# A fused linear-attention and MoE kernel: another order inside a seven-product quarter, and four pieces of side work in other places (blocks 2 to 8)

## The chip, the cores and the metric

The kernel runs on one core of a Trainium2 chip. The metric is the device time of one execution in microseconds (us). Before the change three runs gave 275.19, 275.74 and 276.08 us; the median is 275.74. Engines are called as in the profile: PE is TensorE's matmuls and PEld its weight loads, DVE is VectorE, ACT is ScalarE, POOL is GpSimd, and SP issues most of the DMAs.

## What is computed

For each of 8 batches there is linear attention with 8 heads, 576 tokens and head size 64, and after it a gated layer over all 4608 tokens. Inputs and output are float32; the kernel computes its products in bfloat16 and sums them in float32.

```python
phi = where(x > 0, x, exp(x) - 1) + 1              # of q and k
kv  = k_p^T v                                      # per head, summed over tokens
x   = (q_p kv) / (q_p z + 1e-6)                    # z: sum of k_p over tokens; x is [4608, 512]
h   = x @ w_in                                     # 512 -> 2048
g   = h * sigmoid(beta * h)
out = g @ w_out                                    # 2048 -> 512
```

## The kernel before, in words

**Blocks.** The 576 tokens of a batch are nine groups of 64 rows. Eight of the groups of batch b, 512 tokens, are block b (0 to 7). The ninth groups of all batches, 512 more tokens ("odd tokens", kept in `xT_tail`), are block 8. The loop of L1031 goes over blocks 1 to 8; block 0 is written out ahead of it. Each turn has a phase H (`h_phase` for blocks 1 to 3, `h_fast` for 4 to 8) that computes h and g, and a phase Y (`y_fast`) that computes the output. A schedule is written by hand: every engine runs its instructions in the order in which the code issues them, and the compiler adds the waits. The dictionaries `sh` and `sy` hold side work that is called at a numbered step of H or Y: attention of the next blocks, loads, copies.

**H.** The 16 chunks `ff` of 128 hidden features each take four matmuls of 128x512 (`h_mm`, L402) into one bank of the four-deep ring `hps` and one activation (`silu`, L410) that writes the chunk of g. In blocks 4 to 8 a quarter of the features (chunks 0 to 3; in blocks 7 and 8 also 8 to 11) is computed with seven block products in place of eight (`h_products`, L807). It needs sums and differences of `w_in` (`h_w_sums`, L779, four DVE operations of 128x512 for each quarter) and of x (`h_x_sums`, L793). The products go in four parts between plain chunks. `cw` is a tile of two banks ("hc"), `z` is the first bank of another such tile ("hz"); both are from the ring `wps` of two tiles. Part 1 (L834) ends in two DVE additions that read `cw[:,0]` and `z`; part 2 (L840) ends in L842, which reads `cw[:,1]`; part 3 (L844) accumulates into `cw[:,0]`, `cw[:,1]` and `z`, and DVE adds `h_u[0]` into `cw[:,1]` in place (L848) and into `c2[:,0]` from `z` (L849). `out(0)` (L856) has ACT read `cw` for the quarter's first two chunks, `out(1)` reads `c2`, in SBUF, for the other two.

**The banks behind it.** In blocks 4 to 6, H runs `numer_all` (attention of the next block, L319) after chunk 9 and ahead of chunk 10. Its 72 small matmuls (L333) write first 28 into two banks of `hps`, then the rest into two tiles of `wps`; the first of these takes the place of "hc", so it waits for `out(0)`'s reads. Chunk 10's bank is the one that chunk 8's activation has to read out before. In blocks 7 and 8 a second `h_products` follows the first, and its "hc" takes the place of the first's.

**Y.** Seven products of sixteen 128x256 matmuls (L964): pa, pd, pa, pc, pb, pd, pb. Their left sides are halves of g and sums of them: `g_diff` (L722, one DVE operation of 128x1024 for four chunks) and `g_sums` (L726, three each). DVE forms u2 = pc + r1 (L987) and u3 = pd + u2 (L988); the second product into pd may start when u3 has been formed, since u3 reads pd's bank. Between these lies side work on DVE: `phi` of a later batch (L169, L175), `h_x_sums`, `h_w_sums`.

**POOL.** `tail_copy(b)` (L366) copies the odd tokens of block b from `xT`, which a DMA transpose fills. `next_loads(n)` (L1020) waits, with a tiny copy into `gate`, for another transpose; then it issues the loads of v, q, k for batch n+1 and two conversions of v (L241), which wait for the load.

Of the kernel before, what the change touches and what calls it, by code (L numbers as in the profile page):

```python
# [16 lines left out]
def kernel(  # L17
# [10 lines left out]
    nc = tc.nc  # L28

    B, H, S, D = q.shape  # L30
# [20 lines left out]
    def bank(name, shape=None, dt=F32):  # L51
        return hps.tile(shape or [P, 512], dt, tag="h", name=name)
# [4 lines left out]
    def banks(name, shape=None, dt=F32):  # L57
        return wps.tile(shape or [P, 2, 512], dt, tag="w", name=name)
# [308 lines left out]
    def tail_copy(b):  # L367
        nc.gpsimd.tensor_copy(  # L368
            xT_tail[:, :, b].rearrange("p i r n -> p i (r n)"), xT[b % 2][:, :, 8]
        )  # L370
# [348 lines left out]
    def at(side, n, *fs):  # L719
        side.setdefault(n, []).extend(fs)  # L720

    def g_diff(b, c):  # L722
        g = g_sb[b % 2]
        nc.vector.tensor_sub(gs[2][:, c], g[:, c, 0:HM], g[:, c, HM:512])
# [50 lines left out]
    def h_w_plain(fq, f, r):  # L775

        return w_in_sb[fq][:, 2 * r : 2 * r + 2, f * 256 : (f + 1) * 256]

    def h_w_sums(fq):  # L779

        s, a = h_w[fq], lambda f, r: h_w_plain(fq, f, r)
        nc.vector.tensor_add(s[:, 0], a(1, 0), a(1, 1))
        nc.vector.tensor_sub(s[:, 1], s[:, 0], a(0, 0))
        nc.vector.tensor_sub(s[:, 2], a(0, 0), a(1, 0))
        nc.vector.tensor_sub(s[:, 3], a(0, 1), s[:, 1])

    def h_x_plain(b, r, t):

        if b == B:
            return xT_tail[:, :, 4 * t : 4 * t + 4, r]  # L790
        return xT[b % 2][:, :, 4 * t + r : 4 * t + 4 : 2]
# [15 lines left out]
    def h_products(b, fq):  # L807
        s, t = ([a[:, k] for k in range(4)] for a in (h_w[fq], h_xs))
        cw, z = banks("hc"), banks("hz")[:, 0]
        c2, h_u = h_room("c2"), h_room("h_u")  # L810
        h_u = [h_u[:, 0], h_u[:, 1]]

        def product(ps, lhs, rhs, first):
            for a in range(2):
                for i in range(2):
                    o = ps[:, a * 256 : (a + 1) * 256]
                    m = rhs[:, i]
                    if len(m.shape) > 2:
                        o = o.rearrange("p (t n) -> p t n", n=m.shape[-1])
                    nc.tensor.matmul(  # L820
                        o, lhs[:, i, a * P : (a + 1) * P], m,
                        start=(first and a == 0 and i == 0), stop=True,
                        skip_group_check=True,
                    )

        def w(f, r):
            return h_w_plain(fq, f, r)

        def part0():
            z6 = bank("hz")  # L830
            product(z6, s[1], t[1], True)
            nc.vector.tensor_copy(h_u[0], z6)

        def part1():  # L834
            product(cw[:, 0], w(0, 0), h_x_plain(b, 0, 0), True)
            product(z, s[2], t[2], True)
            nc.vector.tensor_add(h_u[0], cw[:, 0], h_u[0])
            nc.vector.tensor_add(h_u[1], z, h_u[0])

        def part2():  # L840
            product(cw[:, 1], s[0], t[0], True)
            nc.vector.tensor_add(c2[:, 1], cw[:, 1], h_u[1])  # L842

        def part3():  # L844
            product(cw[:, 0], w(0, 1), h_x_plain(b, 1, 0), False)
            product(cw[:, 1], s[3], h_x_plain(b, 1, 1), False)
            product(z, w(1, 1), t[3], False)
            nc.vector.tensor_add(cw[:, 1], cw[:, 1], h_u[0])  # L848
            nc.vector.tensor_add(c2[:, 0], z, h_u[0])  # L849

        def out(n, parts=range(2)):

            for a in parts:
                ff = 4 * fq + 2 * n + a
                src = (cw, c2)[n][:, :, a * 256 : (a + 1) * 256]
                nc.scalar.activation(  # L856
                    g_sb[b % 2][:, ff].rearrange("p (t n) -> p t n", t=2), src,
                    ACTF.Silu, scale=beta_c[:, ff : ff + 1],
                )

        return part0, part1, part2, part3, out

    def h_fast(b, x, side):
        hps_of = {}

        def plain(ff):
            hps_of[ff] = bank("h_ps")
            h_mm(x, ff, hps_of[ff])

        def act(*ffs):  # L870
            for ff in ffs:
                silu(b, ff, hps_of[ff])

        def dual(*ffs):
            for ff in ffs:
                plain(ff)
                act(ff)

        if b < B - 1:
            dual(4)  # L880
            run(side, 0)
        p0, p1, p2, p3, out = h_products(b, 0)
        p0()

        dual(*((5,) if b < B - 1 else (4,)))
        p1()
        dual(*((6,) if b < B - 1 else (5,)))
        p2()
        dual(*((7,) if b < B - 1 else (6,)))
        p3()  # L890
        out(0)
        if b < B - 1:
            dual(8, 9)
            out(1)
            run(side, 9)
            for ff in range(10, FC):
                dual(ff)
                if ff == 10:
                    g_diff(b, slice(0, 4))
                    g_diff(b, slice(4, 8))  # L900
                if ff in (11, 15):
                    g_sums(b, ff - 11, ff - 7)
            return
        run(side, 0)
        dual(7)
        out(1)
        p0, p1, p2, p3, out = h_products(b, 2)
        p0()
        dual(12)
        p1()  # L910
        dual(13)
        p2()
        g_diff(b, slice(0, 4))
        dual(14)
        p3()
        out(0, [0])
        g_diff(b, slice(4, 8))
        dual(15)
        out(0, [1])
        out(1)  # L920
        g_sums(b, 4, 8)
        g_sums(b, 0, 4)

# [96 lines left out]
    def next_loads(b):  # L1020

        for pr in range(2) if b == 2 else ():
            v_copy(nc.gpsimd, b, pr)
        if b + 1 < B:
            nc.gpsimd.tensor_copy(gate, st[b, "qTd"][:, 1, 2 * J - 1, G - 1 : G])
            load_v(b + 1)
            load_qk(b + 1)
            for pr in range(2) if b > 2 else ():
                v_copy(nc.gpsimd, b + 1, pr)

    for b in range(1, B + 1):  # L1031
        n, m = b + 1, b + 2
        sh, sy = {}, {}
        if 2 <= b < B:
            at(sh, 0, lambda: tail_copy(b))
        if n < B:
            at(sh, 0, lambda: next_loads(n))
            at(sh, {1: 9, 2: 2}.get(b, 1 if b == 3 else 0), lambda: kv_both(n))
            at(sh, {1: 11, 2: 5}.get(b, 4 if b == 3 else 9), lambda: numer_all(n))
        if b == 1:  # L1040
            at(sh, 4, lambda: w_sum(2))
            at(sh, 9, lambda: w_sum(1))
            at(sy, 0, lambda: w_sum(3))
        if m < B:
            at(sy, 0, lambda: phi_tile(m, "q"), lambda: phi_tile(m, "k"))
            if b == 1:

                for pr in range(2):
                    at(sy, 0, lambda pr=pr: v_copy(nc.scalar, m, pr))
                for pr in range(2):  # L1050
                    at(sy, 0, lambda pr=pr: phi_exp(m, "q", pr, xin(m, "q", pr)))
                    at(sy, 3 + pr, lambda pr=pr: phi_relu(m, "q", pr, xin(m, "q", pr)))
                    at(sy, 3 + pr, lambda pr=pr: phi_min(m, "q", pr))
                at(sy, 4, lambda: q_trans_dma(m))
                at(sy, 5, lambda: phi_part(m, "k", 0))
                at(sy, 6, lambda: phi_part(m, "k", 1), lambda: table(ACTF.Silu))
            else:
                at(sy, 0, lambda: phi_part(m, "q", 0))
                at(sy, 1, lambda: phi_part(m, "q", 1))
                at(sy, 1, lambda: q_trans_dma(m))  # L1060
                at(sy, 3 if b < 4 else 4, lambda: phi_part(m, "k", 0))
                at(sy, 4, lambda: phi_part(m, "k", 1), lambda: table(ACTF.Silu))
        if b == 2:
            at(sh, 2, lambda: h_w_sums(0))
        if b == B - 2:
            at(sy, 0, lambda: h_w_sums(2))
        if 3 <= b < B:

            for i, step in enumerate((1, 6) if b < B - 2 else (0, 0)):
                at(sy, step, lambda i=i, n=n: h_x_sums(n, range(2 * i, 2 * i + 2)))  # L1070
        (h_phase if b < 4 else h_fast)(b, xT[b % 2] if b < B else xT_tail, sh)
        y_fast(b, sy)

# [29 lines left out]
```

## Time and profile before

| | us |
|---|---|
| median of three runs | 275.74 |
| profiled execution, own time | 275.06 |
| its span, first to last instruction | 273.3 |
| PE busy | 263.6 (96%) |
| DVE busy | 202.8 (74%) |
| ACT busy | 169.2 (62%) |
| POOL busy | 44.2 (16%) |

The profile is of one execution. A row of its timeline gives the start, the duration from the first to the last end (a run of equal instructions is one row, xN), the engine, the line, and in brackets the idle time ahead of it and what ended that. Consecutive matmul rows overlap in the listing since a matmul's end lies after the start of the next; so gaps on PE are read from starts: four 128x512 matmuls take 0.865 us from start to next start, four 128x256 take 0.437, sixteen 128x256 take 1.745. The phases of the later blocks, from PE's rows:

| phase | us from the span's start | length | DVE busy | ACT busy | POOL busy |
|---|---|---|---|---|---|
| H of block 4 | 134.90 to 150.07 | 15.17 | 11.03 | 9.58 | 4.66 |
| Y of block 4 | 150.07 to 162.75 | 12.68 | 11.98 | 8.97 | 0.75 |
| H of block 5 | 162.75 to 178.13 | 15.38 | 11.27 | 9.57 | 4.88 |
| Y of block 5 | 178.13 to 190.81 | 12.68 | 11.98 | 8.98 | 0.58 |
| H of block 6 | 190.81 to 205.99 | 15.18 | 11.27 | 9.58 | 0.00 |
| Y of block 6 | 205.99 to 218.38 | 12.39 | 9.99 | 1.88 | 0.40 |
| H of block 7 | 218.38 to 231.62 | 13.24 | 9.12 | 7.40 | 0.00 |
| Y of block 7 | 231.62 to 243.85 | 12.23 | 9.04 | 3.75 | 0.00 |
| H of block 8 | 243.85 to 257.08 | 13.23 | 9.11 | 7.40 | 0.00 |
| Y of block 8, PE | 257.08 to 269.50 | 12.42 | 8.46 | 3.76 | 0.00 |

### The profile page before, as it was taken

To read this page: it belongs to the slowest core of one execution; us is meant where nothing else is said; L and a number is where in the kernel's file an instruction comes from. 1 tells how busy PE (TensorE), PEld (TensorE's weight loads), DVE (VectorE), ACT (ScalarE), POOL (GpSimd) and SP (SyncE) were. 2 spreads that over 40 slices of the span, in tenths; PEclk is the share of its full clock that TensorE was granted. 3 is DMA by queue.
4 is the path that set the end of the run, shared out by engine and by line. 5 is a ranking of instruction groups with operands and counts; after the bars stand their busy time and mean duration, and the time that the engine had idled before them with its cause. 6 is when DMAs were issued, how large, how long until landed. Compare 5 with 4: busy or idle time off the path is not lost. (4 is left out here: it accounts for less than half of the span.)

```text
span 273.3 us, 6737 instructions
## 1 busy us (share of the span) xinstructions
PE 263.6 (96%) x2840; PEld 179.5 (66%) x2845; DVE 202.8 (74%) x392; ACT 169.2 (62%) x237; POOL 44.2 (16%) x64
## 2 busy tenths in 40 slices
PE   6799999999999999999999999999999999999994
PEld 2575455445865587548864876488648866886793
DVE  4872685999898687557967996799679667856862
ACT  4738897967875875579449933994483047406710
POOL 5923011043004211230113103300000000000000
PEclk9999999999999999999999999999999999999999
DMA  7999999658978996994599568985504050023013
GB/s 251 240 206 352 253 387 248 193 94 241 216 105 174 271 188 116 286 216 62 100 274 228 76 90 234 252 104 86 156 2 86 2 154 4 0 52 104 0 41 115
DMA packets 48958, 42.78 MB, mean 157 GB/s; under 512 B 30352, under 2 KB 40736, under 8 KB 48928
## 3 DMA queue, kind: packets, MB, share of 16 engines
q0 software_dynamic: 13040, 23.40, 36.9%
q1 hardware_dynamic: 35568, 18.75, 32.3%
q8 instruction: 22, 0.36, 0.5%
q10 hardware_dynamic: 320, 0.20, 0.2%
q14 instruction: 8, 0.07, 0.1%
HBM read 36.71 MB, written 9.44 MB: 169 GB/s over the span
## 5 line engine op out<-in xcount | busy, mean ns | idle before, releaser
L410 ACT ACTIVATE g<-h_ps,beta_c 128x512 bf16<-128x512 f32 x116 | 77.6, 688 | 60.7 <-PE h_ps L402 60.4
L402 PE MATMUL h_ps<-xT,w_in 128*128 128x512 bf16 (+1 forms) x480 | 99.8, 358 | 0.1
L402 PEld LDWEIGHTS <-w_in 128*128 128x128 bf16 x512 | 46.7, 98 | 44.0 <-issue 0.2
L964 PEld LDWEIGHTS <-stage 128*128 128x128 bf16 x480 | 46.9, 98 | 5.8 <-issue 0.4
L964 PEld LDWEIGHTS <-g 128*128 128x128 bf16 x384 | 37.5, 98 | 7.1 <-issue 1.1
L964 PE MATMUL ya<-w_out,g 128*128 128x256 bf16 x256 | 30.6, 273 | 0.0
L241 POOL CAST vaug<-vf 128x1152 bf16<-128x1152 f32 x11 | 13.0, 1210 | 38.8 <-DMA vf<-in_v_dram 31.8
L348 DVE TENSOR_TENSOR xs_sb<-nps,rden 128x448 bf16<-128x448 f32 (+2 forms) x24 | 18.2, 758 | 0.8
L162 ACT ACTIVATE e<-xk 128x1152 bf16<-128x1152 bf16 (+1 forms) x15 | 16.7, 1160 | 2.7 <-DMA xk<-in_k_dram 2.7
L162 ACT ACTIVATE e<-xq 128x1152 bf16<-128x1152 bf16 x14 | 15.6, 1159 | 1.6 <-DMA xq<-in_q_dram 1.6
L728 DVE TENSOR_TENSOR stage<-g 128x1024 bf16<-128x1024 bf16 x16 | 11.8, 736 | 6.1 <-ACT g L410 5.8
L964 PE MATMUL yd<-ws,g 128*128 128x256 bf16 x128 | 15.3, 272 | 0.6 <-DVE u L988 0.6
L155 ACT ACT_TABLE_LOAD x12 | 15.4, 1283 | 0.2
L964 PE MATMUL yc<-ws,stage 128*128 128x256 bf16 x128 | 15.3, 273 | 0.0
L964 PE MATMUL yd<-ws,stage 128*128 128x256 bf16 x128 | 15.3, 273 | 0.0
L417 PE MATMUL y_ps<-w_out,g 128*128 128x512 bf16 x60 | 14.6, 379 | 0.3 <-issue 0.2
L175 DVE TENSOR_TENSOR phi_q<-e,r 128x1152 bf16<-128x1152 bf16 x16 | 12.1, 758 | 3.4 <-ACT e L162 2.2
L368 POOL COPY xT_tail<-xT 128x256 bf16<-128x256 bf16 x6 | 2.9, 489 | 70.7 <-DMA xT<-xs_sb 70.7
L175 DVE TENSOR_TENSOR phi_k<-e,r 128x1152 bf16<-128x1152 bf16 x16 | 12.8, 804 | 1.4
L856 ACT ACTIVATE g<-hc,beta_c 128x512 bf16<-128x512 f32 x14 | 9.1, 684 | 7.3 <-DVE hc L848 7.3
L964 PE MATMUL yb<-w_out,stage 128*128 128x256 bf16 x112 | 13.4, 272 | 0.1
L964 PE MATMUL yb<-ws,stage 128*128 128x256 bf16 x112 | 13.4, 273 | 0.0
(135 smaller groups left out, 348.7 us busy)
## 6 DMA issues: line engine op xcount, KB each, us to landing
vf<-in_v_dram POOLq DMA_DIRECT2D x7, 1152.0 KB, 9.0
out_dram<-y SPq DMA_DIRECT2D x29, 256.0 KB, 4.3
xq<-in_q_dram POOLq DMA_DIRECT2D x7, 576.0 KB, 12.0
xk<-in_k_dram POOLq DMA_DIRECT2D x7, 576.0 KB, 14.5
w_in<-in_moe_w_in_dram POOLq DMA_DIRECT2D x4, 512.0 KB, 11.2
g<-in_moe_w_out_dram POOLq DMA_DIRECT2D x2, 1024.0 KB, 16.4
stage<-in_moe_w_out_dram POOLq DMA_DIRECT2D x2, 1024.0 KB, 21.2
stage<-in_q_dram SPq DMA_DIRECT2D x2, 576.0 KB, 4.3
```

What stands on the lines that cost most here:

```text
L155: nc.scalar.activation(act0, warm[:, 0:1], func)
L162: nc.scalar.activation(e, x, ACTF.Exp)
L175: nc.vector.tensor_tensor(st[b, a][:, pr].rearrange("p j (h d) -> p j h d", h=2), st[b, a, pr, "e"].rearrange("p h j d -> p j h d"), st[b, ...
L241: eng.tensor_copy(dst, src)
L348: nc.vector.tensor_mul(xs_sb[:, ils, v0 * D : v1 * D].rearrange("p i (u d) -> p i u d", d=D), pv[:, :, :, 0:D], rden[:, :, :, None].to_bro ...
L368: nc.gpsimd.tensor_copy(xT_tail[:, :, b].rearrange("p i r n -> p i (r n)"), xT[b % 2][:, :, 8])
L402: nc.tensor.matmul(hp[:, c0:c1].rearrange("p (t n) -> p t n", n=n), w_in_sb[ff // 4][:, kc, (ff % 4) * P : (ff % 4 + 1) * P], xm, start=(k ...
L410: nc.scalar.activation(g_sb[b % 2][:, ff, :], hp, ACTF.Silu, scale=beta_c[:, ff : ff + 1])
L417: nc.tensor.matmul(yp[:, c0:c1], g_sb[b % 2][:, ff, t * P : (t + 1) * P], w_out_sb[i][:, c, c0:c1], start=(ff == 0), stop=(ff == FC - 1), ...
L728: nc.vector.tensor_add(gs[0][:, c], g[:, c, HM:512], g[:, c2, HM:512])
L856: nc.scalar.activation(g_sb[b % 2][:, ff].rearrange("p (t n) -> p t n", t=2), src, ACTF.Silu, scale=beta_c[:, ff : ff + 1],)
L964: nc.tensor.matmul(ps[:, p * HM : (p + 1) * HM], lhs(c, p), rhs(c), start=(first and p == 0 and c == 0), stop=True, skip_group_check=True,)
```

## The change

It has four parts. (1) Part 3 of a quarter issues the product into `z` first and the two into `cw` after it; DVE's two additions change places with them. In the second quarter of blocks 7 and 8, `out(1)` goes ahead of `out(0)`. (2) In blocks 4 to 6, `g_diff` of chunks 4 to 7 is issued right after `out(0)`, ahead of chunks 8 and 9 and `numer_all`, in place of after chunk 10. (3) `tail_copy` of blocks 4 to 6 goes behind `next_loads` in POOL's order. (4) `h_w_sums(0)` goes from H of block 2 to H of block 3, and `h_w_sums(2)` in Y of block 6 from the first step to step 4, behind u2, u3 and the first addition into y2.

```diff
         def part3():
+            product(z, w(1, 1), t[3], False)
             product(cw[:, 0], w(0, 1), h_x_plain(b, 1, 0), False)
             product(cw[:, 1], s[3], h_x_plain(b, 1, 1), False)
-            product(z, w(1, 1), t[3], False)
+            nc.vector.tensor_add(c2[:, 0], z, h_u[0])
             nc.vector.tensor_add(cw[:, 1], cw[:, 1], h_u[0])
-            nc.vector.tensor_add(c2[:, 0], z, h_u[0])
...
         out(0)
         if b < B - 1:
+            g_diff(b, slice(4, 8))
             dual(8, 9)
             out(1)
             run(side, 9)
...
                 if ff == 10:
                     g_diff(b, slice(0, 4))
-                    g_diff(b, slice(4, 8))
...
         p3()
-        out(0, [0])
+        out(1, [0])
         g_diff(b, slice(4, 8))
         dual(15)
-        out(0, [1])
-        out(1)
+        out(1, [1])
+        out(0)
         g_sums(b, 4, 8)
...
-        if 2 <= b < B:
+        if 2 <= b < 4 or b == B - 1:
             at(sh, 0, lambda: tail_copy(b))
         if n < B:
             at(sh, 0, lambda: next_loads(n))
+            if b >= 4:
+                at(sh, 0, lambda: tail_copy(b))
...
-        if b == 2:
+        if b == 3:
             at(sh, 2, lambda: h_w_sums(0))
         if b == B - 2:
-            at(sy, 0, lambda: h_w_sums(2))
+            at(sy, 4, lambda: h_w_sums(2))
```

## The prediction

> **What bounds the kernel now.** I read the page first: PE is busy for 263.6 of 273.3 us, at full clock in every slice. Then the chain that ended last: from 187.32 us on it is PE rows (and a few hundredths of issue) until the last addition at 269.55. So time can come only from places where PE stands still, and I looked for these in PE's timeline from 134 us, by starts: a run of four 128x512 matmuls should be followed 0.865 us later, sixteen 128x256 after 1.745.
>
> ```profile
> PE 30%; DVE 1%; issue 0%; DVEq 0%
> ```
>
> The chain is PE; the 1% of DVE is the piece ahead of a wait in block 5. Next, H of block 4 in the timeline of all engines:
>
> ```profile
> 140.04 1.03 PE L402 MATMUL h_ps<-xT,w_in 128*128 128x512 bf16 x4
> 140.24 0.69 DVE L842 TENSOR_TENSOR c<-hc,h_u 128x512 f32<-128x512 f32 x1 [0.25 <-PE hc L820]
> 140.99 0.60 PE L820 MATMUL hc<-xT,w_in 128*128 128x256 bf16 x4
> ...
> 141.86 0.60 PE L820 MATMUL hz<-xs_sb,w_in 128*128 128x256 bf16 x4
> 142.06 0.70 DVE L848 TENSOR_TENSOR hc<-hc,h_u 128x512 f32<-128x512 f32 x1 [1.12 <-PE hc L820]
> 142.29 1.89 PE L402 MATMUL h_ps<-xT,w_in 128*128 128x512 bf16 x8
> 142.67 0.68 DVE L849 TENSOR_TENSOR c<-hz,h_u 128x512 f32<-128x512 f32 x1
> 142.79 1.26 ACT L856 ACTIVATE g<-hc,beta_c 128x512 bf16<-128x512 f32 x2 [1.00 <-DVE hc L848]
> 143.95 1.26 ACT L410 ACTIVATE g<-h_ps,beta_c 128x512 bf16<-128x512 f32 x2
> 144.11 0.83 PE L333 MATMUL nps<-kv_q,qTd 64*64 64x65 bf16 x72
> 144.57 0.17 DVE L346 TENSOR_SCALAR den<-nps 128x7 f32<-128x7 f32 x1 [1.23 <-PE nps L333]
> 144.88 5.35 PE L402 MATMUL h_ps<-xT,w_in 128*128 128x512 bf16 x24
> ```
>
> See part 3 at 140.99: it was due at 140.04 + 0.865 = 140.905. L842 ends at 140.24 + 0.69 = 140.93 and PE goes 0.06 later. Last, PE's own timeline in Y of blocks 4 to 6, and DVE ahead of it in block 4:
>
> ```profile
> 157.06 1.91 PE L964 MATMUL yb<-ws,stage 128*128 128x256 bf16 x16
> 159.26 1.91 PE L964 MATMUL yd<-ws,g 128*128 128x256 bf16 x16 [0.29 <-DVE u L988]
> ...
> 185.12 1.91 PE L964 MATMUL yb<-ws,stage 128*128 128x256 bf16 x16
> 187.32 1.91 PE L964 MATMUL yd<-ws,g 128*128 128x256 bf16 x16 [0.29 <-DVE u L988]
> ...
> 212.98 1.91 PE L964 MATMUL yb<-ws,stage 128*128 128x256 bf16 x16
> 214.89 1.91 PE L964 MATMUL yd<-ws,g 128*128 128x256 bf16 x16
> ```
>
> ```profile
> 155.16 0.75 POOL L368 COPY xT_tail<-xT 128x256 bf16<-128x256 bf16 x1 [8.23 <-DMA xT<-xs_sb]
> ...
> 155.57 0.65 DVE L169 TENSOR_SCALAR r<-xq 128x1152 bf16<-128x1152 bf16 x1
> ...
> 157.80 0.68 DVE L987 TENSOR_TENSOR u<-yc,r 128x512 f32<-128x512 f32 x1
> 158.51 0.69 DVE L988 TENSOR_TENSOR u<-yd,u 128x512 f32<-128x512 f32 x1
> ```
>
> **What PE loses today.** *Y:* yd starts 0.455 late in block 4 (due 158.805), 0.455 in block 5 (due 186.865), 0.165 in block 6 (due 214.725), none in 7 and 8. DVE is the cause: in block 4 its rows follow each other without a break from `g_diff` at 149.04 to u3, which ends at 159.20. *H:* part 3 starts late in all seven quarters by the same reckoning, each time 0.05 to 0.06 after L842's end: 0.085, 0.285, 0.075 (blocks 4 to 6), 0.075 and 0.135 (block 7), 0.075 and 0.135 (block 8), together 0.865. The 0.285 holds 0.20 of chance: one wait instruction of L842 took 222 ns there, where the median is 21. In all PE loses 1.075 + 0.865 = 1.94 us in what the change touches.
>
> **Part 3's new order.** `z` was last read by L838, which ends 0.9 us ahead of part 3 in block 4 (139.30 + 0.69 = 139.99), so `z`'s product can start at once; the `cw` products come 0.437 later, 141.34, when L842 (140.93; 169.00 against 169.20 in block 5) is done. The 0.865 goes. What is late next is `out(0)`. Its addition started 0.20 after the second `cw` product; that product is now last and ends at 142.205. Addition at 142.405, 0.73 to ACT's start (as 142.06 to 142.79): 143.135; two activations with 0.57 between their starts end at 144.40, and chunk 8's runs from 144.295 to 144.985. PE reaches the small matmuls at 144.025; 28 of 72 at 0.0106 bring it to 144.32, where the next bank waits for `out(0)`: 144.40 + 0.05 = 144.45, a wait of 0.13. The other 44 end at 144.92; chunk 10 waits for its bank until 144.985 + 0.05, another 0.12. So 0.25 in each of blocks 4, 5, 6. Chunk 11's bank (chunk 9's activation ends at 145.56, wanted 145.90) and later ones are in time. In blocks 7 and 8 part 1 of the second quarter needs `cw` back: due 226.27 - 0.075 = 226.195, `out(0)` ends at 226.225, start 226.275: 0.08 each. Price 3 x 0.25 + 2 x 0.08 = 0.91. The trace of before shows no such wait, so its ends are: 0 (both banks had 0.24 and 0.36 to spare before, so the wait is only what the shift of 0.43 exceeds), and one whole addition more (0.61) per quarter, below as a rival. I take 0.91, worked from rows that repeat in every block. The other order of `out` at the second quarter's end starts no work later: `c2` is then ready first, chunk 15's activation is no longer behind one on `cw` and the last of the five still ends near 234.2 (234.32 before); pa's second half wants it at 235.11. Nothing.
>
> **g_diff.** One operation of 0.68 (0.60 from start to start) leaves the chain ahead of u3. It goes between L848's end (143.11) and the small matmuls' first DVE row (144.57); chunk 7's g is there since 141.8. It ends near 143.8, so the 1.23 of idle time hides it; if that cover failed, the evacuation would be later by at most 0.60 and the chain no shorter. u3 in block 4 would be ready 0.60 earlier, 158.60, but u2 waits for pc: pc ends at 157.06, u2 0.20 later (as in block 3) and u3 0.72 after that, ending by 158.67. That is under 158.805, by little, so the 0.455 goes; the same sum holds in block 5 (186.73 against 186.865).
>
> **tail_copy.** In block 4's Y the copy ran 0.75 in place of 0.40, and the DVE row beside it 0.65 in place of 0.45. The copy of block 5's odd tokens now follows the conversions (end near 175.8), beside evacuations that kept their 1.09 next to the conversions of block 4. Worth 0.20 on DVE in block 4's Y, where 0.60 suffices already: nothing on PE; bounds -0.20 and +0.20. Block 6's copy still waits for its transpose at 183.4, since `next_loads` issues nothing there. The loads are not moved: POOL waits for the `gate` transpose (8.52 and 8.06) far longer than the copy takes, and `xT`'s buffer is only rewritten two blocks later. *The Trainium skill, page "SBUF — State Buffer", section "Who interferes with whom", says that a DVE operation with two SBUF inputs and a POOL operation that reads SBUF exclude each other; by it the new place is free, because the evacuation reads PSUM, and the sum would be the same.*
>
> **h_w_sums.** Block 3: four operations, 83.00 to 84.47, 1.47 in all, into DVE's idle 2.10 ahead of 112.33: nothing; 0.4 is left. POOL issues k's load beside them (110.10 to 110.87); in block 4 such issues kept 0.75 to 0.76 beside `h_x_sums`. Block 6: u2 gets free by 1.47 and 0.60, more than the 0.165 wants, though `h_x_sums` must wait for the transpose at 210.7. At its new place the work ends at 215.54 + 1.47 = 217.01, so y2's second addition starts 0.17 later than 216.84 and its stores with it; that bank is wanted again at 218.82. Nothing.
>
> *A rule against part 3's gain: the skill's page "PSUM — Partial Sum Buffer", section "PSUM bank collisions raise a hardware error", wants engines kept apart by bank (and by 32 partitions). By that, L842 on `cw[:,1]` has no claim on the product into `cw[:,0]`; the gap would have another cause and might stay, and the sum would be -0.17.* Against it stand seven starts out of seven just behind L842; so the wait is on the whole tile, and I go by the rows.
>
> **Sum.** -1.94 + 0.91 = -1.03, against the profiled execution's 275.06: 274.03. That execution is 0.68 under the median of the runs; taken off the median, 275.74 - 1.03 = 274.7. Differences under about 0.3% (0.83 us) can't be told from none here.
>
> **Rivals.**
> 1. *The new waits don't come* (banks free as early as PE wants them): -1.94, 273.8. For it: the waits hang on 0.1 us; against: the starts are regular to 0.02. Chance 0.14.
> 2. *Y's gain doesn't come*: something else than the shorter chain holds u3, such as a later transpose or `phi` waiting for ACT's exponent (0.54 in block 3): -1.03 + 1.075 = +0.05, 275.8. Against it: no break in DVE's rows of blocks 4 and 5. Chance 0.13.
> 3. *Slower: L849 holds up L848.* If DVE's wait for `z`'s product is only granted when all of part 3 is through, the `c2` addition runs at 142.405 and the `cw` one 0.61 later; PE then waits 0.61 more for banks in five quarters: +3.05 - 1.03 = +2.0, 277.8. It decides as soon as L849 starts after the last `cw` product. Against: L837 starts 0.20 after its own product, with another behind it. Half of that delay gives 276.2. Chance 0.08.
> 4. *The chance 0.20 of block 5 is not there in other runs*: -0.83, 274.9, just at the bound. It is inside the forecast.
>
> **How the numbers follow.** The forecast, 274.3 to 275.1, has 0.65. It puts about six tenths of its chance beyond the bound of 0.83, so faster is 0.65 x 0.62 + 0.14 = 0.54, within 0.3% is 0.65 x 0.38 + 0.13 = 0.38, slower 0.08. The range reaches to rival 1 and to rival 2, 273.8 to 275.9; outside remain rival 3 and the edges.
>
> **What would show it.** Right: part 3's first row is hz, 0.865 after chunk 7's; yd starts 1.745 after pb in blocks 4 to 6; L849 starts ahead of L848; chunk 10 comes 0.1 to 0.3 late behind L333. Wrong: yd still released by u3, or L842 still just ahead of part 3, or chunk 10 late by more than 0.5.

## The result and the profile after

Twelve runs of each kernel gave a median of 274.48 us for the changed kernel and 275.69 for the one before, 1.2 us apart. The ratio of times, taken over all the runs, is 0.9944, with a 95% interval from 0.9923 to 0.9964: 0.6% faster, or 1.0 to 2.1 us. The forecast was 274.7 and -1.03 us.

The two profiled executions alone do not show this: 274.97 us after, 275.06 before. Nearly all of the reason lies ahead of what the change touches. In the changed kernel's execution TensorE was granted 0.74 of its clock from 14 to 20.5 us (1.00 before), and Y of block 1 began at 67.24 us in place of 66.58. Y of block 1 then took 0.30 longer, and blocks 2 and 3 together 0.07; H of block 4 began at 135.90 in place of 134.87 (its first matmul; the table of phases before has 134.90, and so 15.17 in place of 15.20). So I compare lengths of phases from H of block 4 on, which repeat to some 0.04 us from execution to execution. From that start to Y of block 8 it was 122.21 us before and 121.06 after: **-1.15 us**.

In the changed file the two additions of part 3 have changed lines: L848 is now the one from `z` into `c2`, L849 the one into `cw`. First the timeline of the changed kernel in H of block 4. Its columns are as before: start, duration, engine, line.

```profile
141.08 1.03 PE L402 MATMUL h_ps<-xT,w_in 128*128 128x512 bf16 x4
141.28 0.69 DVE L842 TENSOR_TENSOR c<-hc,h_u 128x512 f32<-128x512 f32 x1 [0.25 <-PE hc L820]
141.94 0.60 PE L820 MATMUL hz<-xs_sb,w_in 128*128 128x256 bf16 x4
...
142.58 0.69 DVE L848 TENSOR_TENSOR c<-hz,h_u 128x512 f32<-128x512 f32 x1 [0.61 <-PE hz L820]
142.81 0.60 PE L820 MATMUL hc<-xT,h_w 128*128 128x256 bf16 x4
143.25 1.89 PE L402 MATMUL h_ps<-xT,w_in 128*128 128x512 bf16 x8
143.45 0.70 DVE L849 TENSOR_TENSOR hc<-hc,h_u 128x512 f32<-128x512 f32 x1 [0.18 <-PE hc L820]
144.06 0.68 DVE L724 TENSOR_TENSOR stage<-g 128x1024 bf16<-128x1024 bf16 x1
144.19 1.26 ACT L856 ACTIVATE g<-hc,beta_c 128x512 bf16<-128x512 f32 x2 [1.36 <-DVE hc L849]
145.07 0.83 PE L333 MATMUL nps<-kv_q,qTd 64*64 64x65 bf16 x72
145.34 1.26 ACT L410 ACTIVATE g<-h_ps,beta_c 128x512 bf16<-128x512 f32 x2
...
146.08 5.34 PE L402 MATMUL h_ps<-xT,w_in 128*128 128x512 bf16 x24 [0.18 <-ACT g L410]
```

Part 3 now starts at 141.08 + 0.865, while L842 still runs (it ends at 141.97). The addition from `z` runs under the `cw` products. The addition into `cw` waits for the last of them, and `out(0)` for it. The row of 72 small matmuls lasts 0.83, as before, so nothing holds them. Then chunk 10 starts 1.01 after them where it was 0.77 before: it waits 0.24 for chunk 8's activation (145.34 + 0.69 = 146.03). The view names the releaser, ACT L410. `g_diff` (L724 at 144.06) fits into what was idle time.

Next, PE alone in the changed kernel's Y of blocks 4 to 6:

```profile
158.24 1.91 PE L964 MATMUL yb<-ws,stage 128*128 128x256 bf16 x16
159.99 1.91 PE L964 MATMUL yd<-ws,g 128*128 128x256 bf16 x16
...
185.85 1.91 PE L964 MATMUL yb<-ws,stage 128*128 128x256 bf16 x16
187.60 1.91 PE L964 MATMUL yd<-ws,g 128*128 128x256 bf16 x16
...
213.46 1.91 PE L964 MATMUL yb<-ws,stage 128*128 128x256 bf16 x16
215.20 1.91 PE L964 MATMUL yd<-ws,g 128*128 128x256 bf16 x16
```

Every yd starts 1.75 after its pb, and the brackets with DVE's u are gone. DVE now waits for pc ahead of u2, in block 4 of the changed kernel:

```profile
158.44 0.69 DVE L987 TENSOR_TENSOR u<-yc,r 128x512 f32<-128x512 f32 x1 [0.42 <-PE yc L964]
159.17 0.69 DVE L988 TENSOR_TENSOR u<-yd,u 128x512 f32<-128x512 f32 x1
```

u3 ends at 159.86, 0.13 ahead of yd. That is the small margin that the prediction worked out.

### The profile page after: what moved, and what is told of

It reads as the page before. It is cut to its first block, busy times and chain, and to the rows that moved or that the text cites. A ratio compares the mean times of both kernels' runs of the same rounds, so it can differ in the third digit from the quotient of the medians.

```text
span 273.2 us, 6742 instructions
## 1 busy us (share of the span) xinstructions
PE 265.4 (97%) x2845; PEld 181.3 (66%) x2845; DVE 204.1 (75%) x392; ACT 168.8 (62%) x237; POOL 43.6 (16%) x64
## 4 chain that ended last, share of the span: by engine, by line
PE 79%; DVE 10%; DMA 6%; ACT 2%; issue 1%; SPq 0%; DVEq 0%
PE h_ps L402 30%; PE yd L964 9%; PE ya L964 9%; PE yb L964 8%; PE hc L820 4%; PE yc L964 4%; PE y_ps L417 4%; DMA xT<-xs_sb 4%; PE hz L820 3%; DMA stage<-in_q_dram 2%; PE kvp L223 2%; ACT g L856 1%; PE yb L936 1%; DVE r L169 1%; DVE phi_k L175 1%; DVE xs_sb L348 1%
## 5 line engine op out<-in xcount | busy, mean ns | idle before, releaser
L410 ACT ACTIVATE g<-h_ps,beta_c 128x512 bf16<-128x512 f32 x116 | 77.0, 688 | 58.7 <-PE h_ps L402 58.7
L728 DVE TENSOR_TENSOR stage<-g 128x1024 bf16<-128x1024 bf16 x16 | 12.8, 798 | 5.6 <-ACT g L410 5.6
L724 DVE TENSOR_TENSOR stage<-g 128x1024 bf16<-128x1024 bf16 x16 | 10.9, 682 | 1.9 <-ACT g L410 1.9
```

The source lines that it names most:

```text
L410: nc.scalar.activation(g_sb[b % 2][:, ff, :], hp, ACTF.Silu, scale=beta_c[:, ff : ff + 1])
L728: nc.vector.tensor_add(gs[0][:, c], g[:, c, HM:512], g[:, c2, HM:512])
```

## The experiments

Seven more kernels ran. The side work alone, `g_diff` between and `g_diff` not moved ran once each, so of these only lengths of phases are compared. Lengths of phases in us, from the first start of one phase to that of the next on PE; the sum runs from H of block 4 to the start of Y of block 8.

| | before | changed | order alone | g_diff alone | side work alone | cw[:,1] second | old order in 4 to 6 | g_diff between | g_diff not moved |
|---|---|---|---|---|---|---|---|---|---|
| H 4 | 15.20 | 15.36 | 15.35 | 15.20 | 15.20 | 15.35 | 15.20 | 15.69 | 15.35 |
| Y 4 | 12.68 | 12.22 | 12.45 | 12.23 | 12.48 | 12.23 | 12.22 | 12.22 | 12.24 |
| H 5 | 15.38 | 15.39 | 15.33 | 15.42 | 15.38 | 15.36 | 15.42 | 15.70 | 15.37 |
| Y 5 | 12.68 | 12.22 | 12.24 | 12.23 | 12.68 | 12.23 | 12.23 | 12.22 | 12.44 |
| H 6 | 15.18 | 15.38 | 15.36 | 15.22 | 15.18 | 15.38 | 15.22 | 15.70 | 15.33 |
| Y 6 | 12.39 | 12.23 | 12.22 | 12.23 | 12.22 | 12.22 | 12.23 | 12.23 | 12.23 |
| H 7 | 13.24 | 13.02 | 13.02 | 13.24 | 13.24 | 13.02 | 13.02 | 13.02 | 13.02 |
| H 8 | 13.23 | 13.02 | 13.02 | 13.24 | 13.23 | 13.02 | 13.02 | 13.02 | 13.02 |
| sum against before | 0 | -1.15 | -0.99 | -0.98 | -0.37 | -1.17 | -1.43 | -0.18 | -0.99 |

### The parts alone

**The order of part 3 alone**, on the kernel before:

```diff
         def part3():
+            product(z, w(1, 1), t[3], False)
             product(cw[:, 0], w(0, 1), h_x_plain(b, 1, 0), False)
             product(cw[:, 1], s[3], h_x_plain(b, 1, 1), False)
-            product(z, w(1, 1), t[3], False)
+            nc.vector.tensor_add(c2[:, 0], z, h_u[0])
             nc.vector.tensor_add(cw[:, 1], cw[:, 1], h_u[0])
-            nc.vector.tensor_add(c2[:, 0], z, h_u[0])
...
-        out(0, [0])
+        out(1, [0])
...
-        out(0, [1])
-        out(1)
+        out(1, [1])
+        out(0)
```

> The kernel before with part 1 of the change alone (z's product first, additions changed about, out(1) ahead of out(0) at the end of blocks 7 and 8). Lengths are from PE's starts, against before's profile. Theory (chunk 10 waits for a bank in blocks 4 to 6, and Y's yd hangs on a DVE chain that starts with the small matmuls, so a delay of PE behind them is taken off yd's wait): H of blocks 4, 5, 6 +0.16, 0.0, +0.20; H of 7 and 8 -0.21 each; Y of 4 and 5 -0.25 to -0.30 each, yd still late by 0.15 to 0.2; Y of 6 -0.165; sum about -0.8 us. Rival (H and Y add up independently): the same in H, Y unchanged, sum -0.06 us.

Measured: H +0.15, -0.05, +0.18, -0.22, -0.21; Y of 4, 5, 6 -0.23, -0.44, -0.17; sum -0.99. The ratio of times is 0.9974 (0.9953 to 0.9995). The theory's H holds, and so does the coupling: the waits in H are given back in Y, because DVE's chain to u3 starts with the small matmuls, which come earlier, and PE arrives at yd later. In block 4 the row of small matmuls comes 0.07 earlier after the start of H, and H is 0.15 longer: the 0.23 by which Y is shorter. The rival (-0.06) falls. Y of block 5 was a miss by 0.15 to 0.2: yd was all but in time there. In this execution L169 began 0.05 ahead of POOL's copy and kept its 0.45, and the copy was the one held up (0.66 in place of 0.40). Before, the copy was there first, and L169 took 0.65.

```profile
185.26 0.45 DVE L169 TENSOR_SCALAR r<-xq 128x1152 bf16<-128x1152 bf16 x1
185.31 0.66 POOL L368 COPY xT_tail<-xT 128x256 bf16<-128x256 bf16 x1 [8.06 <-DMA xT<-xs_sb]
...
185.82 0.76 DVE L175 TENSOR_TENSOR phi_q<-e,r 128x1152 bf16<-128x1152 bf16 x1
```

**g_diff alone**, on the kernel before:

```diff
         if b < B - 1:
+            g_diff(b, slice(4, 8))
             dual(8, 9)
...
                     g_diff(b, slice(0, 4))
-                    g_diff(b, slice(4, 8))
```

> The kernel before with g_diff of chunks 4 to 7 moved into H alone. Theory (the chain ahead of u3 gets 0.60 shorter and then u2 waits for pc): H of blocks 4 to 8 as before, part 3 still 0.06 behind L842; yd on time in blocks 4, 5, 6, so Y -0.455, -0.455, -0.165; sum -1.08 us. Rival (something else holds u3, for instance a transpose that lands late): Y of 4 and 5 lose less than 0.2 each, sum under -0.4 us.

Measured: Y -0.45, -0.45, -0.16, H within 0.04 of before, sum -0.98; the ratio is 0.9968 (0.9951 to 0.9985). The theory holds: one operation off DVE's chain removes yd's whole lateness, and part 3 still waits.

**tail_copy and h_w_sums alone**, on the kernel before:

```diff
-        if 2 <= b < B:
+        if 2 <= b < 4 or b == B - 1:
             at(sh, 0, lambda: tail_copy(b))
         if n < B:
             at(sh, 0, lambda: next_loads(n))
+            if b >= 4:
+                at(sh, 0, lambda: tail_copy(b))
...
-        if b == 2:
+        if b == 3:
             at(sh, 2, lambda: h_w_sums(0))
         if b == B - 2:
-            at(sy, 0, lambda: h_w_sums(2))
+            at(sy, 4, lambda: h_w_sums(2))
```

> The kernel before with tail_copy and h_w_sums alone in their new places; the first acts in Y of block 4, the second in Y of block 6. Theory (POOL's copy holds DVE up by 0.20 where it lies beside it, and the chain there is tight): Y of block 4 -0.20, Y of 5 unchanged (that copy has not moved), Y of 6 -0.165, H of 3 unchanged; sum -0.37 us. Rival (the copy only changes places with another wait): Y of block 4 unchanged.

Measured: Y of block 4 -0.20, Y of 5 as before, Y of 6 -0.17, sum -0.37, to the hundredth as expected. H of block 3 was 15.64 against 15.56. In the kernels with the same move it was 15.52 to 15.65, in those without it 15.52 to 15.56, so a cost of up to 0.1 there is neither shown nor ruled out. POOL's copy cost the 0.20 that the row beside it shows, because it stood in the chain that PE waited for. Alone, the three parts give 0.99 + 0.98 + 0.37 = 2.34; together they give 1.15. In Y they remove the same lateness.

### What a wait on a tile covers

On the changed kernel, the two `cw` products exchanged:

```diff
             product(z, w(1, 1), t[3], False)
-            product(cw[:, 0], w(0, 1), h_x_plain(b, 1, 0), False)
             product(cw[:, 1], s[3], h_x_plain(b, 1, 1), False)
+            product(cw[:, 0], w(0, 1), h_x_plain(b, 1, 0), False)
```

> The changed kernel with the two cw products of part 3 exchanged: z, cw[:,1], cw[:,0]; additions as in the changed kernel. It tells what a wait on hc covers. If waits go by the part of the tile that is touched: the addition into cw[:,1] starts 0.26 earlier, right behind the one into c2, out(0) too, chunk 10 is no longer late (its 0.24 goes) in blocks 4 to 6: -0.7 us against the changed kernel, -1.9 against before. If waits go by the whole tile: the addition still starts 0.20 after the last of the products, and all lengths are as in the changed kernel.

Measured: all lengths as in the changed kernel; the ratio to before is 0.9956 (0.9939 to 0.9973). The timeline of this kernel in block 4 shows why:

```profile
142.50 0.60 PE L820 MATMUL hc<-xT,h_w 128*128 128x256 bf16 x4
...
142.94 0.60 PE L820 MATMUL hc<-xT,w_in 128*128 128x256 bf16 x4
143.38 1.89 PE L402 MATMUL h_ps<-xT,w_in 128*128 128x512 bf16 x8
143.58 0.70 DVE L849 TENSOR_TENSOR hc<-hc,h_u 128x512 f32<-128x512 f32 x1 [0.18 <-PE hc L820]
```

`cw[:,1]` is complete at 142.94, yet the addition into it starts at 143.58, 0.20 after the product into the other bank. So DVE's wait goes by the whole tile. PE's wait did the same before the change: part 3's first matmul, which writes the first bank, started just behind L842, which reads the second, seven times out of seven, and with `z`'s product in between it is no longer late.

### A larger dose of the new wait, and the order undone in blocks 4 to 6

On the changed kernel, `g_diff` between the two additions:

```diff
             nc.vector.tensor_add(c2[:, 0], z, h_u[0])
+            if b < B - 1:
+                g_diff(b, slice(4, 8))
             nc.vector.tensor_add(cw[:, 1], cw[:, 1], h_u[0])
...
         if b < B - 1:
-            g_diff(b, slice(4, 8))
             dual(8, 9)
```

> The changed kernel with g_diff of chunks 4 to 7 between the two additions of part 3 in blocks 4 to 6, so that the addition into cw starts some 0.34 us later (143.79 in place of 143.45 in block 4). A dose for the suspected wait. Theory: out(0) and chunk 8's activation go 0.34 later and chunk 10 with them: H of 4, 5, 6 +0.34 each against the changed kernel, Y unchanged. Rival (chunk 10 waits for something other than this chain on ACT): H unchanged.

Measured: H of 4, 5, 6 +0.33, +0.31, +0.32 against the changed kernel, and nothing elsewhere. So the addition's lateness goes through to chunk 10 one to one. In this kernel's block 4 (the addition is L851 here, `out` L858):

```profile
144.62 0.69 DVE L851 TENSOR_TENSOR hc<-hc,h_u 128x512 f32<-128x512 f32 x1
145.34 1.27 ACT L858 ACTIVATE g<-hc,beta_c 128x512 bf16<-128x512 f32 x2 [1.68 <-DVE hc L851]
145.90 1.08 PE L333 MATMUL nps<-kv_q,qTd 64*64 64x65 bf16 x72
...
146.50 1.27 ACT L410 ACTIVATE g<-h_ps,beta_c 128x512 bf16<-128x512 f32 x2
...
146.66 0.20 PEld L333 LDWEIGHTS <-qTd 64*64 64x64 bf16 x15 [0.21 <-issue]
...
147.24 2.10 PE L402 MATMUL h_ps<-xT,w_in 128*128 128x512 bf16 x9 [0.26 <-ACT g L410]
```

Now the small matmuls are held too (1.08 in place of 0.83). The pause shows in their weight loads: the last 16 of the 72 (15 in this row) go on at 146.66, 0.05 after `out(0)` ends (145.34 + 1.27 = 146.61). These 16 write the second of the two `wps` tiles. So the second tile is the one that `out(0)` reads, and the first is not; in the changed kernel `out(0)` is through before the second is wanted.

Then part 3's old order in blocks 4 to 6, the rest as changed:

```diff
         def part3():
+            if b < B - 1:
+                product(cw[:, 0], w(0, 1), h_x_plain(b, 1, 0), False)
+                product(cw[:, 1], s[3], h_x_plain(b, 1, 1), False)
+                product(z, w(1, 1), t[3], False)
+                nc.vector.tensor_add(cw[:, 1], cw[:, 1], h_u[0])
+                nc.vector.tensor_add(c2[:, 0], z, h_u[0])
+                return
             product(z, w(1, 1), t[3], False)
```

> The changed kernel with part 3's old order in blocks 4 to 6 (the new one stays in 7 and 8). Theory (in blocks 4 to 6 the new order buys 0.08 at part 3 and pays 0.24 at chunk 10, because chunk 8's activation stands behind out(0) on ACT): H of 4 and 6 as before, 15.20 and 15.18, that is -0.16 and -0.20 against the changed kernel, H of 5 15.2 to 15.4; H of 7 and 8 13.02; Y 12.22 to 12.24 from block 4 on. Against before -1.45 us from H of block 4 on, against the changed kernel -0.3 to -0.5. Rival (the new order itself is what helps in all blocks): H of 4 to 6 not shorter than in the changed kernel.

Measured: H of 4 and 6 15.20 and 15.22, H of 5 15.42, H of 7 and 8 13.02, Y 12.22 to 12.23; sum -1.43 against before, -0.28 against the changed kernel. The median of twelve runs was 273.43 us against 275.01 for before; the ratio is 0.9944 (0.9923 to 0.9964). By its phases this is the fastest version here. By time alone it can't be told from the changed kernel: both ratios are 0.9944.

### g_diff not moved

On the changed kernel, `g_diff` of chunks 4 to 7 back behind chunk 10:

```diff
         if b < B - 1:
-            g_diff(b, slice(4, 8))
             dual(8, 9)
...
                     g_diff(b, slice(0, 4))
+                    g_diff(b, slice(4, 8))
```

> The changed kernel with g_diff of chunks 4 to 7 back in its old place, behind chunk 10. Theory (the delay of PE by the new order and POOL's moved copy already take nearly all of yd's lateness away): Y of 4 late by at most 0.05, Y of 5 and 6 not late, so all lengths as in the changed kernel within 0.05: g_diff's move adds nothing to the other parts. Rival (the parts add up): Y of 4 and 5 +0.2 or more each.

Measured: Y of 4 and 6 as in the changed kernel (12.24, 12.23), but Y of 5 12.44, late by 0.22; sum -0.99. Half a miss. In block 5 POOL's copy, which the change leaves in Y there, was again ahead of L169, by 0.09:

```profile
183.55 0.43 POOL L368 COPY xT_tail<-xT 128x256 bf16<-128x256 bf16 x1 [7.29 <-DMA xT<-xs_sb]
...
183.64 0.65 DVE L169 TENSOR_SCALAR r<-xq 128x1152 bf16<-128x1152 bf16 x1
```

So with the other parts in place `g_diff`'s move is worth 0.02 in block 4 and, in this execution, 0.22 in block 5. What it buys is room: in the changed kernel the copy beside `h_x_sums` (0.62 in place of 0.42) costs PE nothing.

## Why the prediction was right, step by step

- **What PE loses today: right.** The 1.075 in Y and the 0.865 at part 3 are gone in the changed kernel, seen at each place. The wait at part 3 is on the whole tile, as read from seven starts out of seven. The rule of the Trainium skill that was weighed against it ("PSUM — Partial Sum Buffer", section "PSUM bank collisions raise a hardware error") says what must be kept apart, not what this program's waits cover; the measurement decides.
- **"0.20 of chance" in block 5: wrong.** A wait instruction of 222 to 225 ns ahead of L842 stands in all nine profiles, once in seven, each time in block 5. With the old order H of block 5 was 15.38 to 15.42 in four executions. So rival 4 falls, and the new order hides these 0.20 each time.
- **Chunk 10's wait in blocks 4 to 6: right in size, half right in its path.** 0.25 was forecast; the rows give 1.01 - 0.77 = 0.24 in block 4 and 0.25 in blocks 5 and 6, and the dose moved it one to one. But the step before it was wrong: the first tile of the small matmuls takes the place of "hz", not of "hc" as I described the kernel (the pause in the run with `g_diff` between shows it). The simplest reading is that the ring gives out the tile that was let go first; it fits both places here, but nothing else was tried on it. Its 0.13 did not occur. The sum was not touched, because chunk 8's activation ends later anyway.
- **0.08 in each of blocks 7 and 8: the step of the sum that failed.** Part 1 of the second quarter starts on time (226.51 in block 7), although `out(0)` of the first quarter ends only at 226.54, so its "hc" isn't the tile that `out(0)` reads; by the same reading it lies in the first's "hz" banks. H became 0.22 and 0.21 shorter, not 0.13. The price was 0.24 + 0.25 + 0.25 = 0.74 in place of 0.91.
- **g_diff: right**, by the parts alone (-0.45, -0.45, -0.16). **tail_copy: right**: nothing on top of `g_diff` in block 4, and 0.20 by itself, the bound given. **h_w_sums: right** in block 6, -0.17 by itself; in block 3 no cost stands out from the spread of 0.1.
- **Sum.** -1.94 + 0.74 is -1.20; the phases give -1.15, the forecast was -1.03, the times give -1.0 to -2.1. The first two differ mainly in H of blocks 5 and 6, where the row after the products of k and v now starts 0.76 after theirs in place of 0.71. It does so with `g_diff` alone too; the cause stays open. That forecast and phases lie only 0.12 apart is in small part luck: this loss, which the forecast did not have, makes up for some of the 0.16 that it had too much.
- **Rivals.** 1 fell: the wait at chunk 10 came (at the places in 7 and 8 it did not). 2 fell: nothing else held u3. 3 fell: L848, the addition into `c2`, starts 0.20 after its own product, ahead of the last one.

What stays open is why one wait of L842 takes 0.2 us longer in block 5 in each of these executions.

## What to carry to other kernels

Before adding up the gains of several small edits, write down which late start each of them removes: three edits that were worth 2.34 us one by one gave 1.15 together, since in Y they all removed the same lateness of one product. A reordering that lets the matmuls run on moves the wait to the operation that now comes last; follow that one through the engines to the next bank, and take the new order only where it has room (blocks 7 and 8 here, not 4 to 6). Which tile a ring hands out next did not follow the order of the requests here: find it out rather than count.

## What the runs showed of the hardware that I had not expected

**The granted clock early in the kernel goes with how single executions differ.** From 14 to 20.5 us TensorE was granted 1.00 in three of the nine profiles (before, `g_diff` alone, side work alone), 0.74 or 0.79 in four, 0.53 and 0.51 in those of the order alone and of `g_diff` between the additions. Y of block 1 began at 66.58 to 66.67, at 67.06 to 67.31, and at 68.60 and 68.71 us: later the lower the clock, up to 2.1 us, more than the whole change, in code that is the same in all of them.

**A wait of 0.2 us with a fixed place.** L842's wait instructions in the profile of before and in that of the old order in blocks 4 to 6, two of nine; the figures are the shortest, median and longest in ns:

```profile
L842 DVEq EVENT_SEMAPHORE  x7: 21/21/222, 140.0 to 253.9; - x7
```

```profile
L842 DVEq EVENT_SEMAPHORE  x7: 21/21/223, 140.5 to 253.1; - x7
```

**POOL beside DVE: who starts second waits.** The copy of 0.40 took 0.40 to 0.98 beside DVE rows that read and write SBUF, and such rows gained up to 0.24. L169 went from 0.45 to 0.65, L805 from 0.42 to 0.62. `phi` usually kept its 0.76, but only because it had started first or the copy was nearly done; in the profile of the side work alone, in Y of block 1, it started 0.03 behind the copy:

```profile
79.53 0.40 POOL L368 COPY xT_tail<-xT 128x256 bf16<-128x256 bf16 x1 [15.56 <-DMA xT<-xs_sb]
79.56 0.98 DVE L175 TENSOR_TENSOR phi_k<-e,r 128x1152 bf16<-128x1152 bf16 x1
```

One reading fits all 56 overlaps of such a row with the copy in the nine profiles whose starts lie more than 0.01 apart, to 0.02 us: the row that starts second gets going 0.14 before the recorded end of the first, and then takes its usual time. Here that is 79.93 - 0.14 - 79.56 = 0.23 on top of 0.76. It also gives the 0.20 of L169 and L805 above, and none for the `phi` row at 185.82, since the copy beside it ended at 185.97. So whether the copy costs DVE 0.20 or nothing in a chain that PE waits for hangs on which of the two starts first, by as little as 0.05 (185.26 and 185.31). The Trainium skill, "SBUF — State Buffer", section "Who interferes with whom", says that an operation with two SBUF inputs, as `phi` is, and a copy on POOL hold each other up, and that the later one waits in full. The rows of `phi` and L805 agree, but for the last 0.14 of the first row, which the second does not wait for. L169 has one SBUF input, so that sentence does not speak of it; it was held up in the same way.
